# Random-feature attention and a gated MLP on one core: VectorE operations of the gate/value stage moved onto PSUM operands, GpSimd work moved to VectorE, one of seven products issued later, and the decoding of w_out moved

## The chip, the cores and the metric

The kernel runs on one core of one Trainium2 chip. The metric is the device time of one execution in microseconds. Three runs of the kernel before took 1458.17, 1458.51 and 1461.75 us; the median is 1458.51 us. A difference below about 0.3% (4.4 us) is not told apart from no change.

## The reference

Batch 8, 8 heads, 576 positions, head width 64; 4608 tokens of 512 features, and a gated MLP with 1536 hidden columns.

```python
def phi(x):
    proj = np.einsum('bhsd,df->bhsf', x, w_phi)
    proj = proj - np.max(np.abs(proj), axis=-1, keepdims=True)
    return np.concatenate([np.exp(proj), np.exp(-proj)], axis=-1)
kv  = np.einsum('bhsf,bhsd->bhfd', phi(k), v);  z = np.sum(phi(k), axis=2)
attn = einsum(phi(q), kv) / (einsum(phi(q), z) + 1e-06)
x  = attn as (tokens, features)
xn = x / np.sqrt(np.mean(x * x, axis=-1, keepdims=True) + 1e-06) * rms_g
g  = xn @ w_gate;  val = xn @ w_val
out = (g * sigmoid(g) * val) @ w_out
```

The large weights come in as 64-bit floats, and the kernel decodes them itself.

## The kernel before, in words

The work has four stages, and TensorE is meant to run through all of them.

**Attention.** 32 head pairs run as a software pipeline (front, mid, back, last). Beside them `decode_pieces` turns 64-bit weights into 32-bit ones. A piece loads 128 rows through SP (L37), and `_decode` works on it in order: ScalarE (L48, L49), VectorE (L50 to L52), GpSimd (two halves, L54), VectorE (L55). Pieces of w_gate and w_val either become operands in SBUF (L206, L207) or go back to DRAM through SP (L212).

**Fills.** The first 512 hidden columns of gate and value (4 blocks of 128, `J1`) are multiplied with the not yet normalized x, in slices of `TF` tokens. One unit is 12 matmuls into one of the two banks of the PSUM pool `ps_f` (tiles `fp`, L445), one ScalarE copy (`fo`, L448) and one SP store to the DRAM tensor `gvs` (L449). Some units run inside the attention stage, the rest after it, beside the start of the next stage. The list `ahead` says what is emitted beside these last units.

**Gate/value.** 9 blocks of 512 tokens (`sb`); in each, 8 column blocks `j` of the other 1024 hidden columns. Gate and value of a column block come from one scheme of 7 products with shared sums (Strassen's, in Winograd's form); a product is 6 matmuls of 128x256 (each operand is split into a high and a low part, three matmuls for each of two row chunks). Products 1, 6 and 7 add up in one bank (`pa`), copied out by ScalarE after each (`u`, L645). Product 2 has the bank `pb`. Products 5 and 3 add up in a bank `pe`, product 4 has the bank `pd`. From these VectorE makes the halves of the gate `G` (L655, L671) and of the value `V` (L666, L667). ScalarE applies Silu (L626), VectorE multiplies (L627), SP stores the hidden row block to DRAM. Product 3 of block j comes late: it is held in `pend`, and is emitted inside block j+1. For every second j one of the four filled blocks is read back (`gvr`), multiplied by the row scale `ri` on GpSimd (L678), put through Silu, and multiplied on GpSimd (L627).

`prep` makes the operands of the next token block: load x (L569; the tile has one buffer, so the load waits until the last split has read it), squares and sums (ScalarE, GpSimd), two matmuls with ones (L590, L591), Sqrt on ScalarE (L593), reciprocal and scaling of x on VectorE (L594, L597), sums (L609 to L611, L615), and seven splits into high and low parts (`xo`, 16 buffers; ScalarE casts, L60; VectorE or GpSimd subtracts, L61). The weights of block j are combined and split by `blocks7` (`W`; its staging tiles have one buffer). w_out is decoded in 24 pieces beside sb 1 to 6, and prepared by `load_o` in sb 8.

**Output.** 18 groups of 256 tokens, products with w_out, 126 matmuls each (L814).

The order is not the written one. A list scheduler with its own cost model fixes, before the run, a static order for each engine's queue, from the dependencies and the emission order. Every queue runs strictly in that order: what stands behind a waiting instruction on its engine waits too.

## Time and profile before

| what | value |
|---|---|
| median of 3 runs | 1458.51 us |
| profiled execution: its own time / its span | 1460.03 us / 1458.3 us |
| TensorE busy, matmuls / weight loads | 1309.4 us / 1275.9 us |
| VectorE busy | 1079.7 us |
| ScalarE busy | 798.9 us |
| GpSimd busy | 816.1 us |
| mean granted TensorE clock | 0.963 |
| moved by DMA | 205.76 MB |

All times below are microseconds from the start of the span. A busy time is the sum of an engine's instructions; the TensorE entries are pipelined, so that a matmul's duration is longer than its share of the time (six matmuls with 256 columns, each shown with some 0.3 us, follow each other in 0.71 us). "Idle before, released by" tells what an engine waited for. PEld is TensorE's weight load, which comes just before its matmul and shows the same wait.

The stages in the trace: attention to about 523, the last fills to 697, gate/value to about 1180, output to the end.

### The profile page before, as it was taken

Reading aid. Unit: us, or ns where it says so; the run is one execution under the profiler, and the core shown is the slowest. Engines: PE = TensorE matmul, PEld = TensorE weight load, DVE = VectorE, ACT = ScalarE, POOL = GpSimd, SP = SyncE. Lnnn points to the kernel's source line nnn. Section 1 sums busy time; section 2 is a strip of 40 time slices with the busy share of each in tenths; the row PEclk is TensorE's granted clock in tenths of the full one; section 3 lists DMA queues with packets and bytes.
Section 4 is the critical chain, followed back from the end, with each engine's and each line's share of the span. In section 5 each row is a group of like instructions: output and inputs, shape, how many; then the busy total and the mean of one; then the engine's idle time right before and its main releaser. Section 6 shows DMA issues by size and latency. Waiting matters only on the chain.

```text
span 1458.3 us, 27581 instructions
## 1 busy us (share of the span) xinstructions
PE 1309.4 (90%) x10206; PEld 1275.9 (87%) x10206; DVE 1079.7 (74%) x1513; ACT 798.9 (55%) x1730; POOL 816.1 (56%) x650
## 2 busy tenths in 40 slices
PE   7889999999999986899678788888888879999998
PEld 7889999999999985899578787787788769999998
DVE  7898987777766528510659679779778778999993
ACT  5877987787776744433445545545545444333441
POOL 3764755665444424400455566566555448898883
PEclk9999999999999998999789999999999989999999
DMA  5456676565544253642343453453443344445351
GB/s 155 125 149 158 171 183 174 166 191 164 139 124 119 79 159 117 204 143 95 110 129 122 133 170 111 154 170 110 155 152 108 125 152 130 153 138 173 124 167 44
DMA packets 199143, 205.76 MB, mean 141 GB/s; under 512 B 69280, under 2 KB 152352, under 8 KB 199008
## 3 DMA queue, kind: packets, MB, share of 16 engines
q1 hardware_dynamic: 190432, 199.79, 45.5%
q10 hardware_dynamic: 8576, 4.20, 1.0%
q8 instruction: 81, 1.33, 0.4%
q14 instruction: 54, 0.44, 0.1%
HBM read 130.24 MB, written 73.70 MB: 140 GB/s over the span
## 4 chain that ended last, share of the span: by engine, by line
PE 31%; DVE 9%; issue 6%; DMA 6%; POOL 3%; ACT 2%; ACTq 0%; SPq 0%; POOLq 0%; DVEq 0%
PE gd L814 5%; PE gz L814 5%; PE gy L814 5%; PE fp L445 5%; PE pa L639 4%; DMA x<-xs 3%; PE pe L639 3%; PE fp L814 2%; DVE x L597 2%; DMA gvr<-gvs 1%; PE pd L639 1%; PE pb L639 1%; DVE V L627 1%; DVE xo L61 1%; POOL gvr L678 1%
## 5 line engine op out<-in xcount | busy, mean ns | idle before, releaser
L351 POOL TENSOR_TENSOR ql<-eq,qh 128x256 fp32r<-128x256 f32 x256 | 215.9, 874 | 92.6 <-issue 55.3
L639 PE MATMUL pa<-xo,W 128*128 128x256 f32 x1296 | 202.2, 298 | 46.6 <-ACT u L645 30.0
L639 PEld LDWEIGHTS pa<-xo,W 128*128 128x128 f32 x1296 | 178.8, 202 | 59.1 <-ACT u L645 39.6
L639 PE MATMUL pe<-xo,W 128*128 128x256 f32 x864 | 138.1, 297 | 41.1 <-DVE V L666 29.3
L639 PEld LDWEIGHTS pe<-xo,W 128*128 128x128 f32 x864 | 120.3, 201 | 47.7 <-DVE V L666 33.0
L678 POOL TENSOR_TENSOR gvr<-gvr,ri 128x1024 f32<-128x1024 f32 x36 | 90.5, 2514 | 110.5 <-DMA gvr<-gvs 47.2
L286 DVE TENSOR_REDUCE mx<-pp 128x4 f32<-128x512 f32 (+1 forms) x160 | 100.8, 633 | 67.7 <-PE pp L284 67.1
L61 POOL TENSOR_TENSOR xo<-st,xo 128x768 fp32r<-128x768 f32 x54 | 125.7, 2339 | 45.0 <-ACT xo L60 45.0
L645 ACT COPY u<-pa 128x256 f32<-128x256 f32 x216 | 74.1, 370 | 112.7 <-PE pa L639 109.9
L322 PE MATMUL acc<-vm,ek 128*128 128x65 f32 x1024 | 132.1, 269 | 1.0 <-ACT ek L309 1.0
L445 PE MATMUL fp<-xo,fg 128*128 128x288 f32 x768 | 122.9, 303 | 10.7 <-ACT fo L448 6.7
L322 PEld LDWEIGHTS acc<-vm,ek 128*128 128x128 f32 x1024 | 128.2, 194 | 1.3 <-ACT ek L309 1.2
L445 PE MATMUL fp<-xo,fv 128*128 128x288 f32 x768 | 123.9, 302 | 3.4 <-ACT fo L448 3.2
L445 PEld LDWEIGHTS fp<-xo,fg 128*128 128x128 f32 x768 | 109.4, 193 | 12.4 <-ACT fo L448 7.8
L54 POOL TENSOR_TENSOR wa<-raw,wa 128x256 f32<-128x256 f32 (+1 forms) x96 | 78.2, 834 | 74.4 <-DVE wa L52 50.9
L60 ACT CAST xo<-st 128x768 fp32r<-128x768 f32 x54 | 43.8, 835 | 130.5 <-DVE st L757 60.4
L445 PEld LDWEIGHTS fp<-xo,fv 128*128 128x128 f32 x768 | 109.6, 192 | 4.3 <-ACT fo L448 3.9
L627 DVE TENSOR_TENSOR V<-G,V 128x512 f32<-128x512 f32 x72 | 76.1, 1058 | 35.6 <-ACT G L626 35.6
L61 POOL TENSOR_TENSOR W<-t,W 128x1024 fp32r<-128x1024 f32 x14 | 34.0, 2432 | 120.5 <-ACT W L60 120.5
L347 ACT ACTIVATE qh<-sm 128x512 fp32r<-128x512 f32 (+1 forms) x192 | 96.9, 505 | 0.0
L448 ACT COPY fo<-fp 128x288 f32<-128x288 f32 x128 | 51.2, 405 | 81.3 <-PE fp L445 62.9
L282 PE MATMUL pp<-wh,th 128*128 128x256 f32 x288 | 88.4, 307 | 3.3 <-DVE yr L289 2.1
(156 smaller groups left out, 3657.4 us busy)
## 6 DMA issues: line engine op xcount, KB each, us to landing
ht<-hs SPq DMA_DIRECT2D x18, 1536.0 KB
gvs<-fo SPq DMA_DIRECT2D x128, 144.0 KB
gvr<-gvs SPq DMA_DIRECT2D x36, 512.0 KB
hs<-V SPq DMA_DIRECT2D x72, 256.0 KB
rc<-di SPq DMA_DIRECT2D x32, 288.0 KB
x<-xs SPq DMA_DIRECT2D x16, 576.0 KB
x<-xs SPq DMA_DIRECT2D x9, 1024.0 KB
hs<-gvr SPq DMA_DIRECT2D x36, 256.0 KB
```

Of the source, the lines that this page charges most:

```text
L54: nc.gpsimd.tensor_tensor(a[:, h], lf[:, h], a[:, h], ALU.mult)
L61: (lo_eng or nc.vector).tensor_tensor(lo, x, hi.bitcast(F32), ALU.subtract)
L282: nc.tensor.matmul(o, th[:, cs], wh, start=True, stop=False)
L286: nc.vector.tensor_reduce(mx[:, 0:2 * m], pp[:, 0:2 * m], axis=AX.X, op=ALU.max, apply_absolute_value=True)
L322: nc.tensor.matmul(acc[:, sg, h], e[h][:, sg, j], vm[:, h, j], start=False, stop=(h == 1 and j == T0 - 1))
L347: nc.scalar.activation(hi[:, sg], yi, AF.Exp, scale=1.0 - 2.0 * sg)
L351: nc.gpsimd.tensor_tensor(lo[:, sg, cs], ei[:, sg, cs], hi[:, sg, cs].bitcast(F32), ALU.subtract)
L445: nc.tensor.matmul(fp[:, 0:TF], w, xx[x][:, c], start=(i == 0), stop=(i == 3 * NC - 1))
L627: eng.tensor_tensor(out_, a, v, ALU.mult)
L639: nc.tensor.matmul(o, a, e[:, c], start=(first and c == 0 and i == 0), stop=(c == 1 and i == 2), skip_group_check=True)
L678: nc.gpsimd.tensor_tensor(r, r, xb[sb]["ri"].unsqueeze(1).broadcast_to([128, 2, T]), ALU.mult)
L814: nc.tensor.matmul(place[n], a[:, kp], w[:, o], start=(first and kp == 0 and i == 0), stop=(kp == KP - 1 and i == 2), skip_group_check=True)
```

## The change

Of the code:

- `TF` goes from 288 to 256: 18 fill slices in place of 16, matmuls of 256 columns in place of 288.
- Decode pieces of w_gate and w_val are 256 columns wide in place of 512: 48 pieces in place of 24, at 1.5 per head pair in place of 1. `w2` gets its own buffer.
- The row scale `ri` stays in PSUM: Sqrt, four reciprocals of 128 columns in place of one of 512 (`inverse`), and its readers work on a `ps_f` bank. `prep` has five first steps (squares, scale, inverse, normal, sums) in place of three.
- All seven low-part subtractions of `prep` run on GpSimd (three ran on VectorE); `fourth` changes its sign.
- Products 5 and 4 share a bank `py` (2 buffers), product 3 adds to its second half; V is one addition of 128x512 (L665) in place of two subtractions or additions of 128x256. Silu writes to a PSUM bank `sg` (1 buffer), from which VectorE multiplies (L672).
- Product 3 of block j-1 is emitted after product 4 of block j, not after product 2.
- The filled blocks are scaled on VectorE from the PSUM scale (L680, two instructions of 128x512), not on GpSimd.
- w_out is decoded by pieces in `ahead`, three entries per three fill units (before two), no longer in sb 1 to 6.

```diff
-    TF = S // 2
+    TF = 256
...
-        dq += 1
+        dq += 1.5
...
-    ps_d = gp("g_ps_d", 1, space=PSUM)
-    ps_e = gp("g_ps_e", 2, space=PSUM)
+    ps_y = gp("g_ps_y", 2, space=PSUM)
+    ps_s = gp("g_ps_s", 1, space=PSUM)
...
-            ri = xm.tile([128, T], F32, name="ri", bufs=2)
-            nc.scalar.activation(ri, sp, AF.Sqrt, scale=1.0 / DM, bias=eps)
-            nc.vector.reciprocal(ri, ri)
-            ops["ri"] = ri
+            nc.scalar.activation(sp, sp, AF.Sqrt, scale=1.0 / DM, bias=eps)
+            ops["ri"] = sp
+
+        def inverse():
+            sp = ops["ri"]
+            for c in range(0, T, 128):
+                nc.vector.reciprocal(sp[:, c:c + 128], sp[:, c:c + 128])
+
+        def normal():
             for c in range(NC):
-                nc.vector.scalar_tensor_tensor(x[:, c], x[:, c], g[:, c:c + 1], ri, ALU.mult, ALU.mult)
+                nc.vector.scalar_tensor_tensor(x[:, c], x[:, c], g[:, c:c + 1], ops["ri"], ALU.mult, ALU.mult)
...
-        V, P = nc.vector, nc.gpsimd
-        return [squares, scale, sums], [
-            lambda: split(1, b11, P), lambda: split(2, b21, V),
-            lambda: (split(6, d["t"][1], P), fourth()), lambda: split(5, d["t"][0], V),
-            lambda: split(4, b21, P), lambda: split(7, b12, V), lambda: split(3, b22, P)]
+        P = nc.gpsimd
+        return [squares, scale, inverse, normal, sums], [
+            lambda: split(1, b11, P), lambda: split(2, b21, P),
+            lambda: (split(5, d["t"][0], P), fourth()), lambda: split(6, d["t"][1], P),
+            lambda: split(4, b21, P), lambda: split(3, b22, P), lambda: split(7, b12, P)]
...
+        Y = ps_y.tile([128, 2, HT], F32, name="py")
+        mm(Y[:, 1], 5, True)
+        mm(A, 6, False)
+        u2 = copy(A)
+        mm(Y[:, 0], 4, False)
         while pend:
             pend.pop()()
-        mm(A, 6, False)
-        u2 = copy(A)
-        E = ps_e.tile([128, 512], F32, name="pe")[:, 0:HT]
-        mm(E, 5, True)
-        Dk = ps_d.tile([128, 512], F32, name="pd")[:, 0:HT]
-        mm(Dk, 4, True)
         mm(A, 7, False)
         u3 = copy(A)
-        nc.vector.tensor_tensor(V[:, HT:T], E, u3, ALU.add)
-        nc.vector.tensor_tensor(V[:, 0:HT], u3, Dk, ALU.subtract)
+        nc.vector.tensor_tensor(V.rearrange("p (h t) -> p h t", h=2), Y, u3.unsqueeze(1).broadcast_to([128, 2, HT]), ALU.add)
 
         def third():
-            mm(E, 3, False)
-            nc.vector.tensor_tensor(G[:, HT:T], E, u2, ALU.add)
-            hidden(sb, J1 + j, G, V, V, nc.vector)
+            mm(Y[:, 1], 3, False)
+            nc.vector.tensor_tensor(G[:, HT:T], Y[:, 1], u2, ALU.add)
+            sg = ps_s.tile([128, T], F32, name="sg")
+            nc.scalar.activation(sg, G, AF.Silu)
+            nc.vector.tensor_tensor(V, sg, V, ALU.mult)
...
-        nc.gpsimd.tensor_tensor(r, r, xb[sb]["ri"].unsqueeze(1).broadcast_to([128, 2, T]), ALU.mult)
-        hidden(sb, j, r[:, 0], r[:, 1], r[:, 1], nc.gpsimd)
+        for w in range(2):
+            nc.vector.tensor_tensor(r[:, w], r[:, w], xb[sb]["ri"], ALU.mult)
+        nc.scalar.activation(r[:, 0], r[:, 0], AF.Silu)
+        nc.gpsimd.tensor_tensor(r[:, 1], r[:, 0], r[:, 1], ALU.mult)
...
+    ahead += decode_pieces(decs_late, gp("g_dec", 1))
...
-        now.append(lambda: [ahead.pop(0)() for _ in range(2) if ahead])
+        now.append(lambda: [ahead.pop(0)() for _ in range(3) if ahead])
...
-            if sb and j % 2 == 0 and decs:
-                decs.pop(0)()
```

Three places of the static order. First TensorE's queue in a token block in the middle of the gate/value stage, before. The ten rows are: product 7 of block j-1, 5 of j, 1 of j+1, 3 of j-1, 4 of j (`pd`), 6 of j, 2 of j+1 (`pb`), 5 of j+1, then 18 matmuls of 7 of j, 1 of j+2 and 6 of j+1, and product 3 of j.

```order
L639 MATMUL pa<-xo,W 128x256 x6
L639 MATMUL pe<-xo,W 128x256 x6
L639 MATMUL pa<-xo,W 128x256 x6
L639 MATMUL pe<-xo,W 128x256 x6
L639 MATMUL pd<-xo,W 128x256 x6
L639 MATMUL pa<-xo,W 128x256 x6
L639 MATMUL pb<-xo,W 128x256 x6
L639 MATMUL pe<-xo,W 128x256 x6
L639 MATMUL pa<-xo,W 128x256 x18
L639 MATMUL pe<-xo,W 128x256 x6
```

The same queue of the change. `py` x12 is products 5 and 4 of block j, `pa` x12 is 1 of j+1 and 6 of j, `py` x6 is product 3 of j-1, `pb` 2 of j+1, `pa` x6 is 7 of j, and the last `py` x12 is 5 and 4 of j+1.

```order
L639 MATMUL py<-xo,W 128x256 x12
L639 MATMUL pa<-xo,W 128x256 x12
L639 MATMUL py<-xo,W 128x256 x6
L639 MATMUL pb<-xo,W 128x256 x6
L639 MATMUL pa<-xo,W 128x256 x6
L639 MATMUL py<-xo,W 128x256 x12
```

Between product 7 of a block and its own product 3 there stand two products before (1 and 5, or 1 and 6) and four now (5, 4, 1, 6). Between product 3 of a block and the product 5 that takes over its bank there stand three or four before, and two now.

Second, VectorE's queue where a token block's scale is made and x is scaled, before.

```order
L655 TENSOR_TENSOR G<-pb,u 128x256
L594 RECIPROCAL ri<-ri 128x512
L671 TENSOR_TENSOR G<-pe,u 128x256
L597 SCALAR_TENSOR_TENSOR x<-x,g,ri 128x512 x3
L666 TENSOR_TENSOR V<-pe,u 128x256
L667 TENSOR_TENSOR V<-u,pd 128x256
L597 SCALAR_TENSOR_TENSOR x<-x,g,ri 128x512
L50 TENSOR_SCALAR wp<-wa 128x256
```

And with the change.

```order
L598 RECIPROCAL fp<-fp 128x128 x2
L669 TENSOR_TENSOR G<-py,u 128x256
L598 RECIPROCAL fp<-fp 128x128
L672 TENSOR_TENSOR V<-sg,V 128x512
L598 RECIPROCAL fp<-fp 128x128
L665 TENSOR_TENSOR V<-py,u 128x512
L655 TENSOR_TENSOR G<-pb,u 128x256
L602 SCALAR_TENSOR_TENSOR x<-x,g,fp 128x512 x4
L680 TENSOR_TENSOR gvr<-gvr,fp 128x512 x2
L669 TENSOR_TENSOR G<-py,u 128x256
```

The reciprocals are now spread among the operations on G and V; the decode operation is gone; the scaling of a filled block stands in front of the addition to G that frees the bank `py` (L669).

Third, ScalarE's queue beside the last fills, before: copies of fill results, casts of x, the Sqrt of the first token block's scale, the first cast of a weight block.

```order
L448 COPY fo<-fp 128x288 x9
L60 CAST xo<-x 128x576 x2
L448 COPY fo<-fp 128x288 x12
L593 ACT_TABLE_LOAD
L593 ACTIVATE ri<-fp,eps 128x512
L60 CAST W<-w 128x768
```

And with the change.

```order
L448 COPY fo<-fp 128x256 x2
L49 ACTIVATE raw<-raw 128x256
L448 COPY fo<-fp 128x256
L48 ACTIVATE wa<-raw 128x256
L49 ACTIVATE raw<-raw 128x256
L448 COPY fo<-fp 128x256
L48 ACTIVATE wa<-raw 128x256
L448 COPY fo<-fp 128x256 x3
L60 CAST xo<-x 128x512 x2
```

Many copies out of a fill bank now stand behind decode operations that wait for a piece's load; the 24 pieces lie here, 4 of them beside products of sb 0, 20 beside 46 units that no product interrupts. In the first 15 units after the first Sqrt, all units use one `ps_f` bank, since the other holds the scale of sb 0.

More of the change, by code (lines that the diff above doesn't have):

```diff
@@ L212, in keep @@
             jobs.append((src[at], n, lambda w: nc.sync.dma_start(out=dst[at], in_=w)))
-        for c0 in range(n, DF, 512):
+        for c0 in range(J1 * 128, DF, CH):
             for src, dst in ((w_gate, wgs), (w_val, wvs)):
                 for c in range(NC):
-                    keep(jobs, src, dst, c * 128, c0, 512)
+                    keep(jobs, src, dst, c * 128, c0, CH)
         for j in range(NJ):
@@ L643, in copy @@
         def copy(o):
-            u = wk.tile([128, HT], F32, name="u", bufs=5)
+            u = wk.tile([128, HT], F32, name="u", bufs=6)
             nc.scalar.copy(u, o)
@@ L713 @@
                 first, lasts = prep(sb + 1, fetch(sb + 1), xb[sb + 1])
-            elif 3 <= j < 6 and sb + 1 < NB:
+            elif 2 <= j < 6 and sb + 1 < NB:
                 first.pop(0)()
             elif j == 6 and sb + 1 < NB:
+                first.pop(0)()
                 lasts.pop(0)()
-            if sb and j % 2 == 0 and decs:
-                decs.pop(0)()
             if sb == NB - 1 and 0 < j and len(wos_ops) < KP:
@@ L725 @@
         pend.pop()()
-    assert not decs and len(wos_ops) == KP
+    assert len(wos_ops) == KP
     wos_ops = [(w[:, 0], w[:, 1]) for w in wos_ops]
```

28 lines of the change are left out of this document (12 added, 16 removed).

## The prediction

> **What bounds the kernel now.** I read the stages first. Columns of this view: the stretch, its length, busy time (and count) of PE, PEld, DVE, ACT and POOL, the granted TensorE clock, the DMA share, GB/s.
>
> ```profile
> 200.00:500.00 300.00, 299.87 (x2479) 299.43 (x2479) 217.30 (x363) 223.12 (x549) 154.22 (x183) 1.00 0.54 149
> 633.00:697.00 64.00, 64.00 (x486) 64.00 (x485) 8.63 (x14) 21.29 (x49) 0.00 (x0) 1.00 0.34 114
> 697.00:777.00 80.00, 57.18 (x368) 52.69 (x367) 55.41 (x76) 38.41 (x71) 41.79 (x26) 0.85 0.35 113
> 833.00:1051.60 218.60, 183.20 (x1357) 174.09 (x1356) 181.16 (x275) 110.00 (x237) 132.86 (x97) 0.94 0.44 145
> 1200.00:1440.00 240.00, 240.00 (x2039) 239.99 (x2039) 219.87 (x166) 96.38 (x133) 203.26 (x85) 1.00 0.44 141
> ```
>
> Attention, the last fills and the output keep TensorE busy at a clock of 1.00: there only a change of TensorE's own work can show. What can be won lies between 697 and about 1180. In the four token blocks of 833 to 1051.6 VectorE is busy 45.3 us per block of about 54.7, GpSimd 33.2, ScalarE 27.5, and the clock is 0.94. The chain that ended last gives the period, since x is scaled (L597) once per block:
>
> ```profile
> 645.86 51.20 PE fp L445 x384
> ...
> 776.87 2.43 DVE x L597 x3
> ...
> 1106.31 2.06 DVE x L597 x3
> ...
> 1226.32 4.24 PE gd L814 x36
> ```
>
> Seven such marks, six periods: (1106.31 - 776.87) / 6 = 54.9 us. The two other rows are TensorE undisturbed: 51.20 / 384 = 133.3 ns for a matmul of 288 columns, 4.24 / 36 = 117.8 ns for one of 256. A block has 8 column blocks x 7 products x 6 = 336 matmuls, 39.6 us. Next, what TensorE's weight loads waited for in those four blocks (line, releaser, total us, times, longest):
>
> ```profile
> PEld pa L639 <- ACT u L645: 20.7, 23, 2.7
> PEld pe L639 <- DVE V L666: 12.1, 5, 3.0
> PEld pe L639 <- DVE G L671: 6.4, 6, 1.5
> PEld fp L591 <- POOL sl L61: 3.8, 4, 1.7
> PEld pb L639 <- DVE G L655: 0.9, 2, 0.6
> ```
>
> 43.9 us, 11.0 per block. So a period is 39.6 of products, about 0.5 for the two matmuls with ones, 11.0 of waits, 54.7 x 0.06 = 3.3 from the clock below 1, together 54.4; 0.5 stay unexplained. Two of the waits are named by their view and caused further back: V (L666) is late because it stands behind three scalings of x, and u (L645) because ScalarE stands behind something else, below.
>
> **The gate/value period.** These are the groups by shape in the same four blocks (busy us, mean ns):
>
> ```profile
> L678 POOL TENSOR_TENSOR gvr<-gvr,ri 128x1024 f32<-128x1024 f32 x17 | 42.3, 2490 | 51.4 <-DVE ri L594 25.1 <-DMA gvr<-gvs 13.9 <-issue 7.6
> ...
> L627 DVE TENSOR_TENSOR V<-G,V 128x512 f32<-128x512 f32 x32 | 28.1, 878 | 6.6 <-ACT G L626 6.6
> ...
> L597 DVE SCALAR_TENSOR_TENSOR x<-x,g,ri 128x512 f32<-128x512 f32 x17 | 24.9, 1499 | 0.0
> ...
> L54 POOL TENSOR_TENSOR wa<-raw,wa 128x128 f32<-128x128 f32 x32 | 24.2, 774 | 21.9 <-DVE wa L52 21.9
> ...
> L50 DVE TENSOR_SCALAR wp<-wa 128x256 int32<-128x256 int32 x16 | 20.0, 1253 | 0.0
> ...
> L594 DVE RECIPROCAL ri<-ri 128x512 f32<-128x512 f32 x5 | 16.8, 3353 | 4.2 <-ACT ri L593 4.2
> ...
> L51 DVE SCALAR_TENSOR_TENSOR wp<-wa,wp 128x256 int32<-128x256 int32 x16 | 14.7, 918 | 0.0
> ...
> L55 DVE TENSOR_TENSOR wa<-wp,wa 128x256 f32<-128x256 f32 x16 | 13.1, 818 | 5.9 <-POOL wa L54 5.4
> ...
> L52 DVE TENSOR_SCALAR wa<-wp 128x256 int32<-128x256 int32 x16 | 11.5, 720 | 0.0
> ...
> L61 DVE TENSOR_TENSOR xo<-t,xo 128x512 fp32r<-128x512 f32 x4 | 5.8, 1449 | 0.0
> ...
> L61 DVE TENSOR_TENSOR xo<-x,xo 128x512 fp32r<-128x512 f32 x8 | 5.4, 679 | 0.0
> ```
>
> What these operations cost with a PSUM operand, and a narrow reciprocal, stands elsewhere (count, shortest / median / longest ns; the last row: busy us, mean ns):
>
> ```profile
> L627 DVE TENSOR_TENSOR V<-G,V x72: 677/693/2920, 599.7 to 1177.3; 128x512 f32<-128x512 f32 x72
> L824 DVE TENSOR_TENSOR ro<-gy,os x18: 677/678/692, 1196.9 to 1444.8; 128x512 f32<-128x512 f32 x18
> L396 DVE RECIPROCAL dr<-dr 128x9 f32<-128x9 f32 x11 | 2.3, 212 | 0.9 <-DMA dr<-dd 0.8
> ```
>
> L627 has both operands in SBUF and goes up to 2920 ns; L824 has one in PSUM and stays within 677 to 692, though GpSimd is busy 203 of the 240 us there. So I price the operations that now read PSUM at their undisturbed time. VectorE per block: decoding leaves, (20.0 + 14.7 + 11.5 + 13.1) / 4 = -14.8; L627 at 0.68 instead of 0.88, -1.6; scaling x at about 0.74 instead of 1.50, four times, -3.0; three subtractions to GpSimd, -2.8; V as one operation instead of two, about -0.1. Added: four filled blocks with two operations of 0.68, +5.4; four reciprocals of 128 columns for one of 512: by 212 ns for 9 columns and 3353 for 512, 6.24 ns per column and 156 fixed, 0.96 each, +0.5. Sum -16.4, 45.3 to about 29. GpSimd: -42.3 / 4 = -10.6, -24.2 / 4 = -6.1, + 3 x 1.4 = +4.2, so 33.2 to 20.7. ScalarE loses eight decode operations. All three engines lie far under 39.6 us; the period is then set by TensorE and by single waits.
>
> [...]
>
> Where the waits go, I read from the last full block:
>
> ```profile
> 1061.53 0.71 PE pa L639 x6
> ...
> 1077.33 7.72 DMA x<-xs
> 1085.07 0.63 ACT ss L578
> ...
> 1087.04 1.69 PE pa L639 x12
> ```
>
> - V, 12.1 / 4 = 3.0 per block. Product 3 follows 7 after two products, 2 x 0.71 = 1.4 us; four are 2.8. V must only be read before product 3 enters its bank, and the burst of scalings that V stands behind is 4 x 0.74 = 3.0 instead of 4.2 for three. Only one such burst per block: 0.3 stay. Bounds 0 and 3.0.
> - G (L671, now L669), 1.6 per block. The next product 5 now takes the bank 1.4 us after product 3, before at least 2.1. In the order of the change four scalings of x and two of a filled block, 4 x 0.74 + 2 x 0.68 = 4.3 us, stand in front of one such L669. What is queued behind it is the chain to Silu, nothing of TensorE's but that bank. If the burst begins as product 3 ends the wait is 4.3 + 0.4 - 1.4 = 3.3; if it ends before, 0. I take the middle, 1.7, and 0.3 elsewhere: 2.0. Bounds 0 and 3.6.
> - u, 20.7 / 4 = 5.2. ScalarE's squares of the next x (L578) wait for its load, 7.72 us, and copies u stand behind them. This block has almost no decoding and is 55.4 us long like the others (1050.87 to 1106.31 in the chain), so decoding alone is not what sets it. The load starts when the last split has read the only x tile, and it shares SP's queue with stores of decoded pieces, now gone; against that, seven splits one after another on GpSimd are 7 x 1.4 = 10 us, later than today. I take half, 2.7. Bounds 0.5 and 5.2.
> - Silu writing to PSUM is not in the trace; it delays only the product of G and V, whose V buffers are three. 0; if that cover is gone, its 0.63 us are in the bounds of G.
> - L591: unchanged, 1.0. The three splits that move to GpSimd may come late for their first product: 0.3 (0 to 2).
>
> New period: 39.6 + 0.5 + (0.3 + 2.0 + 2.7 + 1.0 + 0.3 = 6.3) + 0.5 unexplained + 1.9 of clock (3.3 x 6.3 / 11.0) = 48.8. Gain 6.1, times six: **-36.6**.
>
> **Both ends of that stage.** Of 697 to 777, the first part is preparation of weights and stays; the last 37 us run like a period and gain 6.1 / 54.9 = 11%: **-4.1**. Behind 1106.31 the first 27 us gain as much, **-3.0**; then loading of w_out (`load_o`) paces the stage, in steps of
>
> ```profile
> 1153.62 2.41 POOL W L61
> 1156.03 5.39 issue
> ```
>
> 7.8 us, which the change doesn't touch.
>
> **The last fills.** 18 x 256 columns for 16 x 288: 1728 x 117.8 = 203.6 us for 1536 x 133.3 = 204.8, nothing. But the decoding of w_out now lies here, and each copy that empties a fill bank can stand behind it on ScalarE. Engines are idle enough (VectorE 8.63 of 64 us, GpSimd 0); it is the pace that counts. 46 units of 12 x 117.8 = 1.41 us are 65 us, for 20 pieces 3.25 us each. The rows for a piece:
>
> ```profile
> L52 DVE TENSOR_SCALAR wa<-wp x48: 276/422/1112, 21.7 to 1072.5; 128x512 int32<-128x512 int32 x24, 128x256 int32<-128x256 int32 x24
> ...
> L54 POOL TENSOR_TENSOR wa<-raw,wa x96: 455/752/1450, 22.3 to 1074.4; 128x256 f32<-128x256 f32 x48, 128x128 f32<-128x128 f32 x48
> L48 ACT ACTIVATE wa<-raw x48: 419/548/708, 17.2 to 1055.0; 128x512 f32<-128x512 f32 x24, 128x256 f32<-128x256 f32 x24
> ...
> L37 SPq DMA_DIRECT2D raw<-in_moe_w_gate_dram x12: 333/390/584, 13.2 to 271.8; - x12
> ```
>
> The first load is issued at 13.2 and used at 17.2: 4.0 us (of twice the size). Then 0.42 x 2 on ScalarE, three VectorE operations of about 0.4, two halves of 0.455: 6.9 us until the buffer is free, and `raw` has two buffers: 3.5 us per piece, 0.3 over the budget, 20 x 0.3 = +6. To this comes the single fill bank in 15 units (the other holds the scale of the first token block): each may wait for copy and handover, 0.4 us of copy partly hidden, +4 in all. **+10**, bounds 0 and +60 (rival B). In the attention stage 48 pieces of half size cost their engines more, beside a TensorE that is never waited for: 0; the narrower fills shift some 4 us of TensorE's work to before its end and take the same away behind it.
>
> Sum: -36.6 - 4.1 - 3.0 + 10 = -33.7, from the profiled execution's 1460.0: 1426.3. That execution lies 1.5 above the median of the runs: **1425**.
>
> **Rivals.**
>
> A: x's own loop still sets the period: load, squares, Sqrt, four reciprocals, scaling, seven splits on GpSimd, load again, and u waits as long as now. For it speaks that the block without decoding was no shorter; against it that the loop's GpSimd and VectorE parts lose their company. Wait 5.2 instead of 2.7 and clock 2.8: 52.2, gain 2.7: 6 x -2.7 - 3 + 10 = -9, **1450**.
>
> B, slower: decoding paces the last fills. A piece is serial over SP, ScalarE, VectorE, GpSimd and VectorE, and the copies that free fill banks stand in the static order behind its ScalarE steps, SP's stores of `fo` (three buffers) behind its loads. It decides when a piece takes over 3.25 + (43.7 - 4) / 20 = 5.2 us. With VectorE and GpSimd as slow as in the groups above (2 x 0.774 for the halves, 3 x about 0.96) and a load of 6 us beside 114 GB/s of other traffic, a buffer is held 11.3 us, 5.7 per piece: 20 x 2.4 + 4 = +52, in all +9; at 6 us +15. **1472** in the middle. Against it: those two engines are nearly idle there.
>
> C: only TensorE is left. The longer distances hide V and G wholly, u falls to 1.0, the clock rises: 39.6 + 0.5 + 0.5 + 1.0 + 1.0 + 0.6 = 43.2, gain 11.7: -70, -14 at the ends, +4 in the fills: **1379**. For it: all other engines have 10 us of slack; against it: queues are static, and the 4.3 us burst and the x load stay.
>
> **How the numbers follow.** Forecast 0.58, its own range 1402 to 1447; A 0.13; B 0.13; C 0.16. The range 1386 to 1462 leaves out half of C and most of B. A difference under 0.3% (4.4 us) is no change that can be told: 1454 to 1463. Faster: 0.57 of the forecast's share, C whole, 0.07 of A's, as A ends near the bound: 0.80. Same 0.08: the rest of A, a little of B. Slower: 0.12, B.
>
> **What the profile after would show.** The marks of x's scaling (now L602) about 49 us apart; A would show 52, C 43. Waits on V nearly gone from TensorE's list, on u about half, on G (L669) not above 2 us per block. VectorE's busy time per block near 29, L672 near 680 ns. Last fills: TensorE's idle time behind `fo` copies about 10 us; B would show some 55 there. The forecast is wrong if L672 or L680 take well over 0.7 us, or if a wait that is not in today's list (Silu's bank `sg`, splits of x) exceeds 2 us per block.

## The result: 1407.7 us, and the profile after

The changed kernel takes 1407.68 us (median of 4 runs, 1406.96 to 1409.03), the kernel before 1458.34 in the same set: ratio 0.9654, 95% interval 0.963 to 0.9678, that is 50.7 us less. The forecast was 1425, 33.5 less. The profiled execution has a span of 1407.2 us, so the spans differ by 51.1.

I cut both traces at the first of the four scalings of x (L597 before, L602 now) of token block 2 and of the last token block; between them lie six periods.

| part of the span | before | after | difference | forecast |
|---|---|---|---|---|
| start to the mark of token block 2 | 776.8 | 782.3 | +5.5 | +10 - 4.1 = +5.9 |
| six periods | 326.6 (54.4 each) | 279.6 (46.6 each) | -47.0 | -36.6 |
| last mark to the end | 354.9 | 345.3 | -9.6 | -3.0 |

The mark is an operation of VectorE, and TensorE is not at the same product there in both kernels. Its gate/value matmuls (L639, 3024 in each trace) between the marks, before and after (stretch, its length, busy time and count, clock, DMA share, GB/s):

```profile
776.80:1103.40 326.60, 273.13 (x2040) 0.94 0.44 144
```

```profile
782.25:1061.90 279.65, 255.14 (x2019) 0.99 0.41 136
```

So I cut once more by TensorE's own progress. When the last fill ends, 168 of these matmuls are done in both kernels; six blocks are the 2016 from the 673rd on.

| part, by TensorE's count | before | after | difference |
|---|---|---|---|
| start to the end of the last fill | 697.0 | 703.5 | +6.5 |
| from there to the 673rd matmul | 101.3 | 93.7 | -7.6 |
| six blocks | 324.5 | 279.6 | -44.9 |
| behind them | 335.5 | 330.4 | -5.1 |

The six periods between the marks by engine (columns as in the prediction's first view), before and after:

```profile
776.80:1103.40 326.60, 275.48 (x2052) 262.11 (x2051) 263.32 (x407) 161.60 (x349) 191.79 (x139) 0.94 0.44 144
```

```profile
782.25:1061.90 279.65, 256.51 (x2031) 246.92 (x2030) 186.27 (x313) 147.16 (x306) 118.61 (x90) 0.99 0.41 136
```

VectorE has 31.0 us of work per token block instead of 43.9, GpSimd 19.8 instead of 32.0, and the clock is 0.99 instead of 0.94. Then what TensorE's weight loads waited for in the same two stretches (total us, times, longest), before:

```profile
PEld pa L639 <- ACT u L645: 29.6, 33, 2.7
PEld pe L639 <- DVE V L666: 16.8, 8, 3.0
PEld pe L639 <- DVE G L671: 7.8, 7, 1.5
PEld pb L639 <- DVE G L655: 4.2, 5, 2.0
PEld fp L591 <- POOL sl L61: 3.8, 4, 1.7
PEld fp L590 <- ACT sq L60: 0.2, 1, 0.2
```

and after:

```profile
PEld py L639 <- DVE G L669: 13.9, 12, 3.2
PEld pa L639 <- ACT u L645: 6.7, 11, 1.2
PEld py L639 <- DVE V L665: 6.0, 10, 1.3
PEld pb L639 <- DVE G L655: 5.3, 9, 1.1
```

62.4 us became 31.9: 30.5 of the 47.0. The other 16.5 are no waits: 6 x 39.6 = 237.5 us of products at the 117.8 ns a matmul of the output stage (clock 1.00) leave 26.7 us before and 10.2 after for the matmuls with ones, a clock below 1 and, before, the 21 matmuls more between the marks (some 2.5 us). Waits on u and V went, and G's bank became the largest. Which name is the largest does not belong to the change for good, though: with the same gate/value code, c_attn below waits for u again and not for G.

The groups that now read PSUM (same stretch; busy us, mean ns):

```profile
L672 DVE TENSOR_TENSOR V<-sg,V 128x512 f32<-128x512 f32 x49 | 33.7, 687 | 21.1 <-ACT sg L671 20.9
...
L680 DVE TENSOR_TENSOR gvr<-gvr,fp 128x512 f32<-128x512 f32 x48 | 31.1, 683 | 34.6 <-DMA gvr<-gvs 32.6 <-POOL ss L582 2.0
...
L602 DVE SCALAR_TENSOR_TENSOR x<-x,g,fp 128x512 f32<-128x512 f32 x24 | 16.5, 741 | 0.0
```

The same work had means of 878 (L627) and 1499 ns (L597) in the prediction's groups; over the six periods they were 972 and 1345.

In the last fills, TensorE's largest wait is the copy that frees a fill bank:

```profile
PEld fp L445 <- ACT fo L448: 23.7, 25, 2.7
```

ScalarE in turn waited there 20.7 us for loads of pieces and 11.6 for stores of `fo`:

```profile
ACT fo L448 <- PE fp L445: 22.6, 22, 1.9
ACT raw L49 <- DMA raw<-in_moe_w_out_dram: 20.7, 18, 3.3
ACT fo L448 <- DMA gvs<-fo: 11.6, 5, 2.8
```

The kernel before waited there for copies half as long, in the list of TensorE's waits:

```profile
PEld fp L445 <- ACT fo L448: 11.7, 7, 3.0
```

The prediction took TensorE to be busy all through the last fills. Before, that holds from 633 on; ahead of that it does not:

```profile
523.00:633.00 110.00, 83.70 (x552) 79.75 (x551) 57.11 (x64) 44.34 (x88) 43.80 (x24) 0.89 0.51 160
```

With the change it is the other way round: 92.65 us busy at a clock of 0.98 in these 110 us, and behind them, where the kernel before was busy all the time, gaps:

```profile
633.00:703.50 70.50, 61.80 (x481) 59.90 (x482) 30.05 (x80) 31.09 (x85) 16.30 (x36) 0.98 0.64 192
```

So the 6.5 us that the fills end later are a loss less a gain.

Behind the last mark `load_o` works in six steps. GpSimd's part of the first three, before:

```profile
1134.85 2.42 POOL L61 TENSOR_TENSOR W<-t,W 128x1024 fp32r<-128x1024 f32 x1 [0.64 <-ACT W L60]
1145.21 2.40 POOL L61 TENSOR_TENSOR W<-t,W 128x1024 fp32r<-128x1024 f32 x1
1153.62 2.41 POOL L61 TENSOR_TENSOR W<-t,W 128x1024 fp32r<-128x1024 f32 x1 [4.32 <-ACT W L60]
```

and after:

```profile
1088.78 2.69 POOL L61 TENSOR_TENSOR W<-t,W 128x1024 fp32r<-128x1024 f32 x1 [0.38 <-ACT W L60]
1096.73 2.40 POOL L61 TENSOR_TENSOR W<-t,W 128x1024 fp32r<-128x1024 f32 x1 [5.25 <-ACT W L60]
1104.64 2.42 POOL L61 TENSOR_TENSOR W<-t,W 128x1024 fp32r<-128x1024 f32 x1 [4.25 <-ACT W L60]
```

In the kernel before, the first begins 31.4 us behind the mark (1103.4), the next two follow after 10.4 and 8.4 us, then come steps of about 7.8. With the change, the first begins 26.9 us behind the mark (1061.9), and the next two follow after 7.9 us each. So the third begins 50.2 us behind the mark in the kernel before, and 42.7 with the change.

### The profile page after: what moved, and what is told of

Same layout as the page of the kernel before. It is cut to its first block, busy times and chain, and to the rows that moved or that the text cites. A ratio compares the mean times of both kernels' runs of the same rounds, so it can differ in the third digit from the quotient of the medians.

```text
span 1407.2 us, 28525 instructions
## 1 busy us (share of the span) xinstructions
PE 1294.5 (92%) x10398; PEld 1262.7 (90%) x10398; DVE 1032.7 (73%) x1629; ACT 806.7 (57%) x1806; POOL 730.1 (52%) x689
## 4 chain that ended last, share of the span: by engine, by line
PE 26%; DMA 12%; DVE 10%; issue 5%; ACT 3%; POOL 3%; ACTq 0%; SPq 0%; DVEq 0%; POOLq 0%
PE gy L815 5%; PE gd L815 5%; PE gz L815 5%; DMA gvr<-gvs 4%; PE fp L815 3%; PE py L639 2%; DMA x<-xs 2%; PE pa L639 2%; DMA hs<-gvr 2%; DVE gvr L680 2%; PE fp L445 2%; POOL gvr L682 1%; DVE x L602 1%; DMA raw<-in_moe_w_out_dram 1%; DVE fp L598 1%
## 5 line engine op out<-in xcount | busy, mean ns | idle before, releaser
L639 PE MATMUL py<-xo,W 128*128 128x256 f32 x1296 | 186.1, 289 | 24.8 <-DVE G L669 11.4
L639 PE MATMUL pa<-xo,W 128*128 128x256 f32 x1296 | 189.4, 288 | 20.4 <-ACT u L645 9.5
L639 PEld LDWEIGHTS py<-xo,W 128*128 128x128 f32 x1296 | 167.4, 193 | 33.3 <-DVE G L669 14.7
L639 PEld LDWEIGHTS pa<-xo,W 128*128 128x128 f32 x1296 | 170.5, 194 | 28.0 <-ACT u L645 14.2
L54 POOL TENSOR_TENSOR wa<-raw,wa 128x128 f32<-128x128 f32 x144 | 67.8, 492 | 146.1 <-DVE wa L52 74.5
L445 PE MATMUL fp<-xo,fv 128*128 128x256 f32 x864 | 124.7, 287 | 13.3 <-ACT fo L448 13.2
L445 PE MATMUL fp<-xo,fg 128*128 128x256 f32 x864 | 125.3, 289 | 6.1 <-ACT fo L448 5.2
L61 POOL TENSOR_TENSOR xo<-x,xo 128x512 fp32r<-128x512 f32 x45 | 62.5, 1399 | 100.7 <-ACT xo L60 100.7
L448 ACT COPY fo<-fp 128x256 f32<-128x256 f32 x144 | 53.0, 376 | 79.2 <-PE fp L445 50.5
L61 POOL TENSOR_TENSOR xo<-ht,xo 128x768 fp32r<-128x768 f32 x36 | 88.0, 2445 | 0.3 <-ACT xo L60 0.3
L284 PE MATMUL pp<-wh,tl 128*128 128x256 f32 x288 | 85.2, 300 | 2.9 <-DVE tl L61 2.9
```

The source lines that it names most:

```text
L54: nc.gpsimd.tensor_tensor(a[:, h], lf[:, h], a[:, h], ALU.mult)
L61: (lo_eng or nc.vector).tensor_tensor(lo, x, hi.bitcast(F32), ALU.subtract)
L284: nc.tensor.matmul(o, tl[:, cs], wh, start=False, stop=True)
L445: nc.tensor.matmul(fp[:, 0:TF], w, xx[x][:, c], start=(i == 0), stop=(i == 3 * NC - 1))
L639: nc.tensor.matmul(o, a, e[:, c], start=(first and c == 0 and i == 0), stop=(c == 1 and i == 2), skip_group_check=True)
```

## The experiments

The table gives for each run the profiled execution cut at the same marks, the six blocks by TensorE's count, and the median. Runs whose name begins with a_ take one thing back in the changed kernel; with b_, they add one thing to the kernel before; with c_, they are attempts at a better version. The median's scatter is several us for some of them (each time the range of four runs, ten for b_third), and the parts are those of a single execution: for c_half it was the fastest of four, 10.5 us under the median.

An edit moves where the program emits work; the list scheduler then fixes every queue anew. Whether an edit reached the queues has to be read in the trace, and for four of these runs it did not: in a_third_early, a_prep3, b_third and c_attn_te all four engines have, between the marks, the same sequence of operations, tiles and shapes as in the change (the first two), the kernel before and c_attn. These pairs give the scatter of two executions of one order: 279.6, 273.0 and 273.0 us for six periods, 326.6 and 329.9, 276.3 and 275.1. A difference under about 7 us in that column tells nothing.

| run | to the mark | six periods (each) | from the mark | six blocks by count | median us (range) |
|---|---|---|---|---|---|
| before | 776.8 | 326.6 (54.4) | 354.9 | 324.5 | 1458.3 |
| the change | 782.3 | 279.6 (46.6) | 345.3 | 279.6 | 1407.7 (1407.0 to 1409.0) |
| a_third_early | 786.2 | 273.0 (45.5) | 348.3 | 272.9 | 1409.6 (1405.9 to 1416.0) |
| a_decode_gv | 769.5 | 294.3 (49.1) | 347.5 | 291.4 | 1413.3 (1407.8 to 1416.8) |
| a_ri_sbuf | 789.1 | 282.9 (47.2) | 356.3 | 282.3 | 1432.7 (1430.1 to 1435.9) |
| a_scale_pool | 793.1 | 287.9 (48.0) | 356.0 | 285.9 | 1436.1 (1430.4 to 1443.3) |
| a_gvbody | 785.0 | 284.3 (47.4) | 352.9 | 278.4 | 1423.7 (1422.6 to 1426.5) |
| a_split_v | 782.5 | 284.2 (47.4) | 349.9 | 282.6 | 1418.1 (1413.0 to 1418.9) |
| a_prep3 | 783.7 | 273.0 (45.5) | 347.4 | 273.0 | 1404.6 (1401.4 to 1406.9) |
| b_third | 776.9 | 329.9 (55.0) | 353.2 | 327.5 | 1460.3 (1456.6 to 1466.8) |
| b_decode | 778.3 | 296.6 (49.4) | 362.3 | 296.3 | 1440.4 (1437.2 to 1445.6) |
| c_attn | 785.7 | 276.3 (46.1) | 348.4 | 276.2 | 1411.2 (1408.5 to 1416.2) |
| c_attn_te | 786.5 | 275.1 (45.9) | 348.9 | 275.0 | 1410.7 (1408.5 to 1412.7) |
| c_half | 774.8 | 279.8 (46.6) | 346.9 | 278.7 | 1413.9 (1403.4 to 1424.2) |

### Product 3: distance or company?

The prediction gave the end of the waits on V to the distance between products 7 and 3. First the change with product 3 early again, a_third_early:

```diff
         nc.vector.tensor_tensor(G[:, 0:HT], Bk, s1, ALU.add)
+        while pend:
+            pend.pop()()
         Y = ps_y.tile([128, 2, HT], F32, name="py")
...
         mm(Y[:, 0], 4, False)
-        while pend:
-            pend.pop()()
         mm(A, 7, False)
```

> The change, with product 3 of block j-1 emitted after product 2 again, as before; all else of the change stays. Theory D (distance: the wait for V went because product 3 comes four products after 7): the wait on V returns at the bank of products 5 and 3, with 2 to 3 us per token block, and the time rises by 12 to 20 us, to 1420 to 1428. Theory C (company: V was late because VectorE's operations were stretched by GpSimd and queued behind decoding; without these the old distance is enough): at most +4 us, 1408 to 1412.

Measured 1409.6, ratio 0.9656 (0.9616 to 0.9696) against 0.9654: no difference. But this is TensorE's queue in that run:

```profile
891.55 1.60 PE L639 MATMUL py<-xo,W 128*128 128x256 f32 x12
892.99 1.60 PE L639 MATMUL pa<-xo,W 128*128 128x256 f32 x12
894.43 0.84 PE L639 MATMUL py<-xo,W 128*128 128x256 f32 x6
895.11 0.88 PE L639 MATMUL pb<-xo,W 128*128 128x256 f32 x6
895.83 0.88 PE L639 MATMUL pa<-xo,W 128*128 128x256 f32 x6
```

It is the queue of the change, and so are all 2016 matmuls between the marks: with product 3 emitted early, the scheduler made the same order. The run is the change executed once more, there are four products between 7 and 3 in both, and theory D is not tested. What it shows is scatter: 273.0 us for six periods at a clock of 1.00 and with 27.8 us of waits, where the change's profile had 279.6, 0.99 and 31.9. The wait on V is 5.9 us, against 6.0. Then the other direction, product 3 late in the kernel before, b_third:

```diff
-        while pend:
-            pend.pop()()
-        mm(A, 6, False)
-        u2 = copy(A)
         E = ps_e.tile([128, 512], F32, name="pe")[:, 0:HT]
         mm(E, 5, True)
+        mm(A, 6, False)
+        u2 = copy(A)
         Dk = ps_d.tile([128, 512], F32, name="pd")[:, 0:HT]
         mm(Dk, 4, True)
+        while pend:
+            pend.pop()()
         mm(A, 7, False)
```

> The kernel before, with product 3 of block j-1 emitted after product 4 of block j; nothing else. Theory D (distance, the term of the prediction): most of the 3.0 us of waiting for V per token block goes, period 54.4 to about 52, 1440 to 1448. Theory L, after the run that put product 3 back at no cost: what waits for V waits elsewhere for the same late VectorE, period within 1 us, 1452 to 1464.

Measured 1460.3, ratio 1.0002 (0.9981 to 1.0024): nothing. Here too the order between the marks is that of the kernel before, on all engines, so that the wait on V in a second execution is all that it shows, 16.8 us in the first:

```profile
PEld pe L639 <- DVE V L666: 20.9, 12, 3.0
```

Whether the distance between products 7 and 3 ends the waits on V stays open. What the runs do show is that the place where product 3 is emitted does not make that distance: the scheduler arrives at four products in the change with either place, and at the old order in the kernel before.

### Decoding of w_out

Back beside token blocks 1 to 6 in the change, a_decode_gv:

```diff
-    ahead += decode_pieces(decs_late, gp("g_dec", 1))
...
-        now.append(lambda: [ahead.pop(0)() for _ in range(3) if ahead])
+        now.append(lambda: [ahead.pop(0)() for _ in range(2) if ahead])
...
+    decs = decode_pieces(decs_late, dec)
...
+            if sb and j % 2 == 0 and decs:
+                decs.pop(0)()
```

> The change, with w_out decoded beside token blocks 1 to 6 again, two entries of the list beside the last fills per three units as before. Theory D: the wait on u (1.1 us per token block now, 5.2 before) partly returns, period 46.6 to about 48.5, +11 us over six periods, and the last fills lose most of their 24 us of waits on copies, -12 to -18: 1401 to 1408. Theory C, with the decoding as the largest part of VectorE's queue: period back to 51 or more, +26 and more, against the same gain in the fills: 1416 or more.

Measured 1413.3, between the two expectations. Six periods +14.7 us, the part before them -12.8, the part behind +2.2, so the move is worth about 4 us in the trace once all else is changed, and 5.6 by the medians, of which the scatter leaves little. In the fills the waits on copies are 17.2 us instead of 23.7; the other 6 of the 12.8 were not isolated (the part before the marks differs by 3.9 us between the change and a_third_early, whose orders are equal there). Alone in the kernel before, with TF of 256 to make room for its buffers, b_decode:

```diff
-    TF = S // 2
+    TF = 256
...
+    ahead += decode_pieces(decs_late, gp("g_dec", 1))
...
-        now.append(lambda: [ahead.pop(0)() for _ in range(2) if ahead])
+        now.append(lambda: [ahead.pop(0)() for _ in range(3) if ahead])
...
-            if sb and j % 2 == 0 and decs:
-                decs.pop(0)()
```

> The kernel before, with the decoding of w_out beside the last fills (three entries of the list per three units) and TF of 256; nothing else. Undoing this in the change cost 2.45 us per token block and gave back 12.8 in the fills. Additive theory: period 54.4 to 52, fills +13, time 1453 to 1461. Theory L (the parts help each other: as long as the old work of GpSimd and VectorE is there, less load gives more): period to 50 or less, 1435 to 1448.

Measured 1440.4, ratio 0.9872 (0.9831 to 0.9912): 19.4 us less than before in that set. The six periods are 30.0 us shorter, twice what taking it back cost; ahead of them 1.5 and behind them 7.4 are lost. By rows of that stretch, u is not what became better:

```profile
PEld pa L639 <- ACT u L645: 36.0, 42, 3.5
PEld pe L639 <- DVE V L666: 9.2, 6, 1.8
PEld pe L639 <- DVE G L671: 2.6, 4, 0.7
```

```profile
778.30:1074.90 296.60, 259.25 (x2029) 248.07 (x2029) 195.17 (x314) 149.13 (x307) 160.76 (x97) 0.98 0.39 128
```

Waits sum to 47.8, 14.6 less than before; the clock went from 0.94 to 0.98, and 23 of the gate/value matmuls (2.7 us) lie no longer between the marks; that is the other half. VectorE's load fell from 43.9 to 32.5 us per block. The waits on VectorE's results (V and both halves of G) fell from 28.8 to 11.8 us, of which V from 16.8 to 9.2. VectorE's other operations became only somewhat faster: the mean of the product of G and V went from 972 to 953 ns, that of the scaling of x from 1345 to 1169, some 5 us over the 48 and 24 of them, so less company from GpSimd explains a part at most. A shorter queue on VectorE is the likely cause of the rest; but the scheduler also made another order for TensorE's queue, and the run does not separate the two.

### Operands in PSUM, and GpSimd's company

One place of the kernel before and one after, in the order of time (start, us):

```profile
784.96 2.93 POOL L678 TENSOR_TENSOR gvr<-gvr,ri 128x1024 f32<-128x1024 f32 x1 [3.28 <-DMA gvr<-gvs]
785.55 2.89 DVE L627 TENSOR_TENSOR V<-G,V 128x512 f32<-128x512 f32 x1
```

```profile
1047.86 1.29 DVE L680 TENSOR_TENSOR gvr<-gvr,fp 128x512 f32<-128x512 f32 x2 [1.97 <-POOL ss L582]
1047.88 1.28 POOL L582 TENSOR_TENSOR ss<-ss,sq 128x512 f32<-128x512 f32 x1 [0.74 <-ACT sq L581]
```

L627, both operands in SBUF, lasts 2.89 us beside GpSimd's operation of 2.93; two L680, one operand in PSUM, take 1.29 us together beside a GpSimd operation of 1.28. In the whole trace before, 29 of the 72 products L627 took over 0.8 us, and each of them overlapped work of GpSimd; of the 72 L672 after, 34 lay beside GpSimd for more than half of their time, and none took over 693 ns. What that is worth, I asked by undoing it. The old block body in the change, a_gvbody (product 4 in a bank of its own, V from two operations, Silu in SBUF):

```diff
-        Y = ps_y.tile([128, 2, HT], F32, name="py")
-        mm(Y[:, 1], 5, True)
+        E = ps_e.tile([128, 512], F32, name="pe")[:, 0:HT]
+        mm(E, 5, True)
...
-        mm(Y[:, 0], 4, False)
+        Dk = ps_d.tile([128, 512], F32, name="pd")[:, 0:HT]
+        mm(Dk, 4, True)
...
-            sg = ps_s.tile([128, T], F32, name="sg")
-            nc.scalar.activation(sg, G, AF.Silu)
-            nc.vector.tensor_tensor(V, sg, V, ALU.mult)
+            nc.scalar.activation(G, G, AF.Silu)
+            nc.vector.tensor_tensor(V, G, V, ALU.mult)
```

> The change, but the block body of before: product 4 in a bank of its own, V from two operations of 128x256, Silu in place in SBUF, V multiplied from two SBUF operands; product 3 late as in the change. Theory P (the PSUM operands of G and V are what shortens the period, since operations with SBUF operands alone are held up by GpSimd): the product of G and V back to about 0.88 us or more, VectorE +3 us per token block, period from 46.6 to 49 or more, 1420 to 1430. Theory L (the load that left VectorE and GpSimd is what counts, and their operations now rarely meet): product at about 0.70, period 46 to 47.5, 1404 to 1413.

Measured 1423.7, ratio 0.9757 (0.9722 to 0.9792), 16 us slower than the change. The product has its long instances back (mean 926 ns, 687 in the change):

```profile
L673 DVE TENSOR_TENSOR V<-G,V 128x512 f32<-128x512 f32 x49 | 45.4, 926 | 25.7 <-ACT G L672 25.7
```

The product is held up again, as theory P has it, and the time is in its range. The period is not: 47.4 lies in that of theory L. Of the 4.7 us in six periods nothing is left by TensorE's own count, 278.4 against 279.6, since it has more matmuls between the marks here:

```profile
785.00:1069.30 284.30, 259.44 (x2060) 0.99 0.40 135
```

The 16 us lie ahead of the 673rd matmul (804.4 us, 797.2 in the change) and behind the 2689th (339.4, 330.4). The run also undoes the joined addition for V and the shared bank, so that it does not price the PSUM operand alone.

The row scale in SBUF instead of PSUM, a_ri_sbuf, and with it the filled blocks on GpSimd again, a_scale_pool:

```diff
-            nc.scalar.activation(sp, sp, AF.Sqrt, scale=1.0 / DM, bias=eps)
-            ops["ri"] = sp
+            ri = xm.tile([128, T], F32, name="ri", bufs=2)
+            nc.scalar.activation(ri, sp, AF.Sqrt, scale=1.0 / DM, bias=eps)
+            ops["ri"] = ri
```

> The change, but the row scale is written to SBUF by the Sqrt, so that the reciprocals, the scalings of x (L602) and of the filled blocks (L680) on VectorE have all operands in SBUF. Theory C by operand (operations with all operands in SBUF are held up by GpSimd): mean of L602 and L680 rises from 0.74 and 0.68 us to 1.0 or more, VectorE +3 us or more per token block, period +1 to +2, time +6 to +12, 1414 to 1420. Theory C by load (GpSimd is simply less busy now) and theory D: the durations stay within 10%, and 1404 to 1411; the fill bank freed for the first units may give back 2 to 4 us.

```diff
-        for w in range(2):
-            nc.vector.tensor_tensor(r[:, w], r[:, w], xb[sb]["ri"], ALU.mult)
+        nc.gpsimd.tensor_tensor(r, r, xb[sb]["ri"].unsqueeze(1).broadcast_to([128, 2, T]), ALU.mult)
```

> As the run with the scale in SBUF, and the filled blocks are scaled on GpSimd again (one operation of 128x1024, four per token block). Theory C: GpSimd's 2.5 us operations stretch VectorE's operations with SBUF operands (scalings of x to about 1.5 us, copies of V and G delayed): period +3 to +5, 1425 to 1438. Theory D: GpSimd at about 31 of 47 us per token block is no bound, VectorE loses 5.4 us of work per block, period within 1 us: 1402 to 1414.

Measured 1432.7 and 1436.1; the ratios, 0.9817 (0.9777 to 0.9857) and 0.9836 (0.9788 to 0.9883), overlap. The first is 25 us slower than the change (21 in the profiled execution, the fastest of its four), more than any theory had; but its scalings of x were not held up (744 ns against 741), those of the filled blocks somewhat (823 against 683). The periods lost 3.3 us, no more than scatter. Outside the periods, 6.8 us are lost before the mark and 11.0 behind the last one, and TensorE's list of waits shows one long wait in each part:

```profile
PEld fp L590 <- ACT sq L60: 15.9, 1, 15.9
```

before the first token block (no wait of more than 4 us stands there in the change), and

```profile
PEld fp L816 <- ACT xo L60: 12.1, 1, 12.1
```

before the output (6.8 in the change). At the first, TensorE's queue stands at the matmul with ones until ScalarE has cast the squares. That is a wait of this kernel's static order, and no longer duration of an operation; why the order came out so, and whether the place of the scale must bring it, stays open. In the second run GpSimd's long operations are back beside scalings of x, and these are held up as in the kernel before:

```profile
L603 DVE SCALAR_TENSOR_TENSOR x<-x,g,ri 128x512 f32<-128x512 f32 x24 | 27.1, 1187 | 0.0
```

The operation and its operands are those of the first run, 744 ns there; what differs is that the filled blocks are scaled on GpSimd. The period is 0.8 us longer than in the first run, which is within the scatter. Theory C (held up by operand, where GpSimd works from SBUF at the same time) is shown in the durations (means of 1187 and 744 ns; GpSimd's scaling of the filled blocks, L680 in the second run, has a mean of 2439); that it makes the 25 us is not.

### Splits, and the steps of the preparation

a_split_v puts three low-part subtractions back on VectorE:

```diff
-            lambda: split(1, b11, P), lambda: split(2, b21, P),
-            lambda: (split(5, d["t"][0], P), fourth()), lambda: split(6, d["t"][1], P),
-            lambda: split(4, b21, P), lambda: split(3, b22, P), lambda: split(7, b12, P)]
+            lambda: split(1, b11, P), lambda: split(2, b21, nc.vector),
+            lambda: (split(5, d["t"][0], nc.vector), fourth()), lambda: split(6, d["t"][1], P),
+            lambda: split(4, b21, P), lambda: split(3, b22, P), lambda: split(7, b12, nc.vector)]
```

> The change, with three of the seven low-part subtractions of the next token block's x on VectorE again. Theory L: VectorE +2 to 3 us per token block at 31 to 34 of 47: period +0.5 to +1, 1410 to 1416. Theory that GpSimd's ten us of splits in a row delay the next load of x: period -0.5 to -1.5, 1397 to 1405.

Measured 1418.1, ratio 0.9705 (0.9662 to 0.9749), 10 us slower than the change: +0.8 us per period, the size that theory L had but within the scatter, and 4.6 behind the last mark. Taking three splits off GpSimd did not shorten anything, so the theory that ten us of splits in a row delay the next load has nothing for it. a_prep3 makes the operands in three steps, as before:

```diff
-        return [squares, scale, inverse, normal, sums], [
+        return [squares, lambda: (scale(), inverse(), normal()), sums], [
...
-            elif 2 <= j < 6 and sb + 1 < NB:
+            elif 3 <= j < 6 and sb + 1 < NB:
...
-                first.pop(0)()
                 lasts.pop(0)()
```

> The change, but the operands of the next token block are made in three steps as before: ones, Sqrt, four reciprocals and four scalings of x in one step, from j = 3 on. Theory B (burst: what stands in VectorE's queue in one piece delays G, Silu behind it on ScalarE, and u behind Silu): 7 us in one piece, waits on u from 1.1 to 3 or more per token block, period +1.5 to +2.5, 1417 to 1424. Theory L (only the sum of the work counts, which is the same): period within 0.5, 1405 to 1411.

Measured 1404.6, ratio 0.9601 (0.9569 to 0.9632): not slower; the interval overlaps that of the change by a hair, so I call it no difference. Between the marks the scheduler made the same order of every queue as in the change, with the reciprocals spread out, so there was no burst, and theory B is not tested. What the run shows is that emitting in five steps instead of three brings nothing there: the queues come out the same.

### Attempts at a better version

c_attn decodes all of w_out in the attention stage, c_attn_te does so with product 3 early:

```diff
-    decs = decode_pieces(early, dec)
+    decs = decode_pieces(early + decs_late, dec)
...
-        dq += 1.5
+        dq += 2.25
...
-    ahead += decode_pieces(decs_late, gp("g_dec", 1))
...
-        now.append(lambda: [ahead.pop(0)() for _ in range(3) if ahead])
+        now.append(lambda: [ahead.pop(0)() for _ in range(2) if ahead])
```

> The change, with all of w_out decoded in the attention stage (2.25 pieces per head pair instead of 1.5), none beside the last fills, there two entries of the list per three units. If idle time of VectorE, ScalarE and GpSimd there takes 24 more pieces beside a TensorE that stays busy: the 24 us of waits on copies in the fills fall to about 11, period as in the change, 1392 to 1400. If the attention stage's engines fall behind TensorE by them (VectorE is busy 72 of 100 us there): attention 5 to 20 us longer, 1400 to 1420.

> As the run with all of w_out decoded in the attention stage, and product 3 after product 2, as before. By the run that moved product 3 back alone (+1.9 us, inside its scatter, with a period of 45.5 instead of 46.6 and 7 us more at both ends): within 4 us of the run without it. Theory D would have it 12 us slower.

Measured 1411.2 and 1410.7, ratios 0.9655 (0.9625 to 0.9685) and 0.9647 (0.9622 to 0.9673): equal to each other and to the change. The two have the same order between the marks, so product 3 is not tested here either. c_attn's waits in the six periods are 28.5 us, as in the change, under other names:

```profile
PEld pa L639 <- ACT u L645: 25.6, 33, 1.6
PEld py L639 <- DVE V L665: 2.9, 7, 0.4
```

The waits on copies fell from 23.7 to 15.6 us in the fills, but TensorE lost about as much while attention starts up, in the stretch from 100 to 200 us of c_attn

```profile
100.00:200.00 100.00, 86.56 (x668) 83.61 (x668) 87.36 (x172) 76.85 (x201) 57.69 (x85) 0.95 0.59 160
```

and of the change

```profile
100.00:200.00 100.00, 92.87 (x707) 90.52 (x705) 85.60 (x167) 78.35 (x200) 58.44 (x82) 0.91 0.55 141
```

668 matmuls instead of 707 (703 and 734 in a_third_early and a_decode_gv, whose attention code is that of the change). c_half, on top of a_prep3, puts 12 pieces beside the fills and 12 beside the token blocks:

```diff
-    ahead += decode_pieces(decs_late, gp("g_dec", 1))
+    pieces = decode_pieces(decs_late, gp("g_dec", 1))
+    ahead += pieces[:12]
+    decs = pieces[12:]
...
+            if sb and j % 4 == 0 and decs:
+                decs.pop(0)()
```

> The change with the operands made in three steps (the run that did this alone took 1404.6), and the decoding of w_out shared out: 12 pieces beside the last fills at two entries of the list per three units, 12 in token blocks 1 to 6, two per block. If either place has slack that the first pieces use for nothing: waits on copies in the fills from 24 to about 14 us, period 45.5 to at most 46.5, 1394 to 1401. If each piece costs the same wherever it stands (about 0.6 us by the runs so far): 1401 to 1408.

Measured 1413.9, with runs from 1403.4 to 1424.2, ratio 0.971 (0.9661 to 0.9759): inconclusive, and no gain. Its fills still wait 22.5 us for copies, with half the pieces. None of the three beats the change beyond doubt.

## Why the prediction was right, and where its steps failed

**Place and sign** were right: attention and output did not move, the last fills cost something, the six periods gave the gain. 1407.7 lies in the range (1386 to 1462) and inside the forecast's own (1402 to 1447), between the forecast (1425) and rival C (1379). Of the mechanism, the runs show the decoding's part and the prices of the operations; the reasons given for V and u are not shown, and that the sum came within 17 us owes something to luck.

**The step that was too small: the period, 46.6 measured, 48.8 forecast, from 54.4 by the first scaling (54.9 by the chain's marks).** The sum of the waits was nearly right, 6.3 forecast and 31.9 / 6 = 5.3 measured, from 10.4. By name: G 2.0 forecast, 2.3 measured; u 2.7 and 1.1; V 0.3 and 1.0; the sum of squares (L591) 1.0 and 0; L655, which I left out, 0.9. Another 0.5 is the term called unexplained: the chain's last mark, 1106.31, is not the first scaling of its block, which starts at 1103.4. From first scaling to first scaling the period is 54.4, which is what the sum had given. What failed most is the clock: I let its loss shrink with the waits, from 3.3 to 1.9; it went to 0.99, about 0.5, and everything that is neither product nor wait, 2.9 in the forecast, fell from 4.5 (0.4 of it the marks) to 1.7 us per period. b_decode shows that this does not follow the sum of the waits: with 47.8 us of waits it had 0.98 already.

**The step whose size was nearly right and whose reason is not shown: V.** I forecast a fall of 2.7 us per block, from 3.0 to 0.3; it was 1.8, from 2.8 to 1.0. I gave it to the four products of distance and to the shorter burst of scalings. No run tested the distance, since the scheduler undid both edits. What the runs show is that V's wait falls from 16.8 us (20.9 in a second execution of that order) to 9.2 when only the decoding leaves. That load I had counted (VectorE forecast 29 us per block, measured 31.0; GpSimd 20.7 and 19.8), and had let load off the path cost next to nothing.

**u** I gave half to the stores and the decoding that leave. Alone that move did not help u at all (36.0 us against 29.6). In the change, taking one part back raises it from 6.7 to 23.6 us (decoding, the first row below) or 14.2 (body, the two rows after it).

```profile
PEld pa L639 <- ACT u L645: 23.6, 28, 2.5
```

```profile
PEld pe L639 <- DVE V L666: 15.4, 16, 2.0
PEld pa L639 <- ACT u L645: 14.2, 23, 1.5
```

But c_attn, which takes nothing back in this stage, has 25.6 on u, and the body's run has 32.3 us of waits in all, as much as the change: what u and V gained there, G's banks lost. With another order of the queues the waits go to other names. What made u's wait fall is not shown.

In the six periods only the decoding costs more than the scatter when it is undone (14.7); body 4.7, splits 4.6, scale in SBUF 3.3 and GpSimd's scaling 5.0 lie within it, and together all are 32.3 of 47.0. In the whole time the same undoings cost 5.6, 16.0, 10.5, 25.0 and 3.4, some 60 us and more than the gain of 50.7. The parts do not add up either way, and how the gain in the periods divides among them, beyond the decoding, stays open.

**Prices** held: 687 ns for the product with a PSUM operand (0.68 forecast), 741 for scaling x (0.74), 683 for the filled blocks (0.68), and the narrow reciprocal, interpolated as 0.96, was

```profile
L598 DVE RECIPROCAL fp<-fp x36: 952/966/967, 557.2 to 1060.4; 128x128 f32<-128x128 f32 x36
```

At the median, an operand in PSUM made no difference to the product: L672 with one in PSUM has 691 ns, L627 with both in SBUF 693.

**Up to the mark of token block 2** the part is 5.5 us longer, 5.9 forecast, and that agreement is in part luck. The fills end 6.5 us later, not 10; TensorE's waits on their copies are 23.7 us, where I had expected about 10, but 11.7 of them were there before, in the 110 us that I had taken for busy. From the end of the fills to the mark the change takes 1.0 us less and does 34 matmuls (4.0 us) more: a gain of 5.0, 4.1 forecast. The 4.0 us do not appear in the part, because the mark now comes later in TensorE's work. Rival B did not come.

**Behind the last mark** I forecast -3.0 and got -9.6 (-5.1 by TensorE's count). 7.5 us of it lie ahead of `load_o`'s third step: 4.5 ahead of the first, 3.0 in the first two steps, which took 10.4 and 8.4 us before and not the 7.8 that I had read from a later one. Which part of the change brings that was not isolated; undoing the scale in PSUM, the body or the splits gives 11.0, 7.6 and 4.6 of it back.

## What to carry to other kernels

Where VectorE and GpSimd both work from SBUF, look at the longest duration of a VectorE operation beside its shortest (2920 and 677 ns here); with one operand in PSUM the same product had no such tail (673 to 693 ns). Load on an engine that is never the longest can still cost: 24 pieces of decoding were worth 30 us of the token blocks, with VectorE at 81% of the time, and 19.4 us of the whole. Where a scheduler fixes the queues, compare the queues of two runs before reading a difference of their times: four edits here changed the emission and left the order of the stage as it was. They were worth something all the same, as repeats: they show how far two executions of one order differ. And a named wait tells who was late in that order, not which edit will help.
